# Fused attention, gated MLP and residual MLP on one core: nine of 24 head pairs transpose p on TensorE, in PSUM banks shared with the mixing MLP

## The chip, the cores and the metric

The kernel runs on one core of a Trainium2 chip. The metric is the device time of one execution in microseconds (us); the median of three runs of the kernel before is 1159.89 us (1159.18 to 1160.92). PE is TensorE, DVE is VectorE, ACT is ScalarE, POOL is GpSimd, SP is SyncE, which here issues most DMAs.

## The reference

Three stages follow each other, with B = 4 batches, S = 448 positions, H = 12 heads of D = 64, model width 768:

```python
q_n, k_n = (rmsnorm(q, g_q), rmsnorm(k, g_k))
scores = scale * np.matmul(q_n, k_n.transpose(0, 1, 3, 2))
scores = scores - np.max(scores, axis=-1, keepdims=True)
attn = np.exp(scores)
attn = attn / (np.sum(attn, axis=-1, keepdims=True) + 1e-09)
x = np.matmul(attn, v)                      # then heads side by side: [B, S, 768]

h = np.maximum(x @ w_in, 0.0)               # w_in [768, 1024]
u, v = (h[..., :d_ff // 2], h[..., d_ff // 2:])
v_n = (v - mu) / np.sqrt(var + 1e-06)
v_s = np.einsum('ts,bsd->btd', w_spatial, v_n) + b_spatial[None, :, None]
x = (u * v_s) @ w_out                       # w_out [512, 768]

xn = (x - mu) / np.sqrt(var + 1e-06) * g_ln
out = x + np.maximum(xn @ w_ch1, 0.0) @ w_ch2   # w_ch1 [768, 3072], w_ch2 [3072, 768]
```

The first stage is called attention here, the second the mixing MLP, the third the channel MLP.

## The kernel before, in words

Most products are made in f16 with each operand split into a high and a low half, so one product is three f16 products (high by high, high by low, low by high).

**Attention** goes by 24 pairs of heads, six to a batch. `att_slot` (L346) handles pair i and finishes pair i-1. `s_mm` (L231) makes the scores of a pair in four groups of two, two, two and one blocks of 128 rows (two heads of 64 rows); `softmax1` (L245) takes the row maximum on DVE (L251) and the exponential on ACT (L256), giving p in f32, unnormalised. To multiply p by v, p must be transposed. `softmax2` (L261) has two ways. For the pairs in `PE_PAIRS` (L228, pairs 0 to 5) each block of p is transposed in f32 by four PE transposes (L270) into a PSUM tile of the pool `ps_t`, and ACT copies it to SBUF (L271); `av_mm` (L284) then multiplies by v in f32 (L293). For the other pairs ACT makes the high half of p (L275), DVE the low half (L276), SP issues a DMA transpose (L278), POOL scales and splits v (L219, L221) with ACT between them (L220), and `av_mm` uses 22 f16 matmuls (L300).

`av_scale` (L304) brings 1/sum to the layout of the product: DVE multiplies the reciprocals by a 64x64 identity repeated twice (tile `dg`, L314, laid out as half, block n, row q), PE sums it over partitions (L319), ACT copies the result to `rb` (L321). `av_out` (L324) multiplies the product in PSUM by `rb` (L332); both are ordered block by block, and the result is written row by row, so both inputs are read with a step of 64 elements.

**The mixing MLP** is `moe1` (L570), one call per batch: v part (psv, L591), u part (psu, L613), spatial mixing (pss, four groups, L631 and L633), output product (pso, L650 and L660). Each group of matmuls takes one bank of the PSUM pool `ps_m`, which has two buffers; ACT or DVE empties it. Its weights are 64-bit words in DRAM that DVE decodes (L420 to L422) and splits (L397). `moe1_weights` runs beside pairs 0 to 6; `moe1` of batch b (0 to 2) beside pairs 6b+7 to 6b+12; `moe1` of batch 3 runs after attention, beside the layer norm and the first products of the channel MLP. That split is written in `merge` (L35) and the code at L1142 to L1148.

**The channel MLP** (`ffn1` L708, `ffn2` L765) follows, with its matmuls at L729 and L780 and its weight preparation at L420 to L422, L536 and L537.

**PSUM** has eight banks: `ps_x` 1, `ps_o` 1, `ps_s` 4 (two tiles of two banks), and 2 that belong to `ps_t` until pair 6's slot is over and then to `ps_m`:

```python
    c.wraw.release()
    c.ps_t.release()
    c.ps_m = ps_m = pool("ps_m", "left", 2, space=PSUM)
    c.m1 = pool("m1", "right", 1)
```

Tiles of one pool and tag take their buffers in the order in which the program names them.

**The order on each engine** is not that of the code. `issue_order` (L1056) lists all instructions, and `schedule` (L986) sorts them per engine by priorities and estimated costs. The priorities are perturbed in the steps of the table `SHAKES` (L815): seed, spread, passes. Each engine then executes its list strictly in that order.

Of the kernel before, what the change touches and what calls it, by code (L numbers as in the profile page):

```python
# [10 lines left out]
F16 = mybir.dt.float16  # L11
BF16 = mybir.dt.bfloat16
F32 = mybir.dt.float32
I32 = mybir.dt.int32
AF = mybir.ActivationFunctionType
ALU = mybir.AluOpType
AX = mybir.AxisListType
PSUM = bass.MemoryType.PSUM
DRAM = bass.MemoryType.DRAM

P = 128
B, H, S, D = 4, 12, 448, 64
NB = 7
# [131 lines left out]
def att_load(c, i):  # L155
# [9 lines left out]
    nc.sync.dma_start(out=vr[64:128, :, 0:6, :], in_=vs[:, :, 1:7, :])  # L165
    if i not in PE_PAIRS:
        nc.sync.dma_start(out=vr[64:128, :, 6, :], in_=vs[:, :, 0, :])
# [43 lines left out]
def att_v(c, i):  # L211

    nc = c.nc
    p = c.pr[i]
    if i in PE_PAIRS:
        return
# [8 lines left out]
GROUPS = ((0, 1), (2, 3), (4, 5), (6,))  # L225

CHUNKS = (0, 128, 256, S - 128)
PE_PAIRS = {0, 1, 2, 3, 4, 5}  # L228


def s_mm(c, i, g):  # L231
# [29 lines left out]
def softmax2(c, i, g):  # L261

    nc = c.nc
    p = c.pr[i]
    n = len(GROUPS[g])
    if i in PE_PAIRS:
        for j, blk in enumerate(GROUPS[g]):
            pt = c.ps_t.tile([P, 512], F32, tag="ps_t", name=f"ps_t{i}_{blk}")
            for ch, k0 in enumerate(CHUNKS):
                nc.tensor.transpose(pt[:, ch * P:(ch + 1) * P], p.pe[g][:, j, k0:k0 + P], c.ident[:])  # L270
            nc.scalar.activation(p.pT[:, blk * 512:(blk + 1) * 512], pt, AF.Copy)  # L271
        return
    x = p.pe[g][:, 0:n]
    p16 = c.att.tile([P, 2, 2, S], F16, tag="p16", name=f"p16_{i}_{g}", bufs=3)
    nc.scalar.activation(p16[:, 0:n, 0], x, AF.Copy, scale=2.0 ** 14)  # L275
    nc.vector.scalar_tensor_tensor(p16[:, 0:n, 1], x, 2.0 ** 14, p16[:, 0:n, 0], op0=ALU.mult, op1=ALU.subtract)  # L276
    b0 = GROUPS[g][0]
    nc.sync.dma_start_transpose(out=p.pT[:].bitcast(F16)[:, b0 * NB * P:(b0 + n) * NB * P].rearrange("p (c q) -> p c q", q=P),  # L278
                                in_=p16[:, 0:n].rearrange("p b t k -> p (b t k)"))


def av_mm(c, i):
# [4 lines left out]
    p.po = c.ps_o.tile([P, 512], F32, tag="ps_o", name=f"ps_o{i}")  # L287
    if i in PE_PAIRS:
        pT = p.pT.rearrange("p (b c q) -> p b c q", b=NB, c=4)
# [14 lines left out]
def av_scale(c, i):  # L304

    nc = c.nc
    p = c.pr[i]
    nc.vector.tensor_scalar(p.sm, p.sm, 1e-9, None, op0=ALU.add)
    nc.vector.reciprocal(p.sm, p.sm)
    s16 = c.small.tile([P, 2, NB], F16, tag="s16", name=f"s16_{i}", bufs=2)  # L310
    nc.vector.tensor_scalar(s16[:, 0], p.sm, 2.0 ** 15, None, op0=ALU.mult)
    nc.vector.scalar_tensor_tensor(s16[:, 1], p.sm, 2.0 ** 15, s16[:, 0], op0=ALU.mult, op1=ALU.subtract)
    dg = c.att.tile([P, 2, NB, 64], F16, tag="dg", name=f"dg{i}", bufs=1)
    nc.vector.tensor_tensor(dg.rearrange("p t n q -> p (t n) q"),  # L314
                            s16.rearrange("p t n -> p (t n)").unsqueeze(2).to_broadcast([P, 2 * NB, 64]),
                            c.eye2[:].unsqueeze(1).to_broadcast([P, 2 * NB, 64]), op=ALU.mult)
    pr = c.ps_o.tile([P, 512], F32, tag="ps_o", name=f"ps_r{i}")
    for t in range(2):
        nc.tensor.matmul(pr[:, :S], c.head, dg[:, t].rearrange("p n q -> p (n q)"), start=(t == 0), stop=(t == 1))  # L319
    p.rb = c.att.tile([P, S], F32, tag="rb", name=f"rb{i}", bufs=1)  # L320
    nc.scalar.activation(p.rb, pr[:, :S], AF.Copy, scale=2.0 ** -15 if i in PE_PAIRS else 2.0 ** -29)  # L321


def av_out(c, i):  # L324
    nc = c.nc
    p = c.pr[i]
    b, hp = i // NPAIR, i % NPAIR
    if hp == 0:
        c.xT[b] = c.xpools[b % 2].tile([P, NC6, 2, S], F16, tag="xT", name=f"xT{b}")
    xT = c.xT[b]  # L330
    x = c.att.tile([P, S], F32, tag="xo", name=f"xo{i}", bufs=1)
    nc.vector.tensor_tensor(x.rearrange("d (p n) -> d p n", n=NB), p.po[:, :S].rearrange("d (n p) -> d p n", n=NB),  # L332
                            p.rb.rearrange("d (n p) -> d p n", n=NB), op=ALU.mult)
    if i in PE_PAIRS:
        split(c, x, xT[:, hp, 0, :], xT[:, hp, 1, :], c.sv[b][:, 0:1])
    else:
        nc.scalar.activation(xT[:, hp, 0, :], x, AF.Copy)
        nc.vector.tensor_tensor(xT[:, hp, 1, :], x, xT[:, hp, 0, :], op=ALU.subtract)
    del c.pr[i]
# [6 lines left out]
def att_slot(c, i, n):  # L346
# [7 lines left out]
    if i < n:  # L354
        p = c.pr[i]
        p.ps, p.pe = {}, {}
        p.pT = c.att.tile([P, NB * 4 * P], F32, tag="pT", name=f"pT{i}", bufs=2)
        s_mm(c, i, 0)
        yield S_COST[0]
        softmax1(c, i, 0)  # L360
        s_mm(c, i, 1)
        yield S_COST[1]
        softmax1(c, i, 1)
        softmax2(c, i, 0)
    if i < n:
        s_mm(c, i, 2)
        yield S_COST[2]
        softmax1(c, i, 2)
        softmax2(c, i, 1)
    if i % 2 and i + 2 < n:  # L370
        att_front(c, i + 2, min(2, n - i - 2))
    if i > 0:
        av_scale(c, i - 1)
        av_mm(c, i - 1)
        yield AV_COST
        av_out(c, i - 1)
    if i < n:
        s_mm(c, i, 3)
        yield S_COST[3]
        softmax1(c, i, 3)  # L380
        softmax2(c, i, 2)
        softmax2(c, i, 3)
# [11 lines left out]
def split(c, raw, hi, lo, scale):  # L394

    c.nc.scalar.activation(hi, raw, AF.Copy, scale=scale)  # L396
    c.nc.vector.scalar_tensor_tensor(lo, raw, scale, hi, op0=ALU.mult, op1=ALU.subtract)  # L397
# [399 lines left out]
def weave(a, b):  # L797

    out = [iter(a), iter(b)]
    while out:  # L800
        for g in list(out):
# [10 lines left out]
WINDOW = 3413  # L812


SHAKES = ((0, 0, 2), (556, 3000, 2), (1748, 20000, 1), (1711, 1000, 3), (1453, 8000, 1), (1124, 20000, 1), (257, 300,  # L815
# [3 lines left out]


def free_size(ap):
# [225 lines left out]
def issue_order(tc):  # L1047
# [3 lines left out]
    prio = [float(o.n) for o in g.ops]  # L1051
    for seed, spread, passes in SHAKES:
        rnd = random.Random(seed)
# [13 lines left out]
def kernel(ctx: ExitStack, tc: tile.TileContext, q, k, v, g_q, g_k, w_in, w_spatial, b_spatial,  # L1067
                                   w_out, g_ln, w_ch1, w_ch2, out):
    nc = tc.nc
    c = Ctx()  # L1070
# [8 lines left out]
    def pool(name, side, bufs=1, **kw):  # L1079
        return tc.alloc_tile_pool(name=name, bufs=bufs, side=side, reuse_waits="tile", **kw)  # L1080
# [4 lines left out]
    dram = pool("dram", "left", space=DRAM)  # L1085
    c.x2d = dram.tile([B * S, DM], F32, name="x2d")
    c.ps_x = pool("ps_x", "left", 1, space=PSUM)
    c.ps_t = pool("ps_t", "left", 2, space=PSUM)
    c.ps_o = pool("ps_o", "right", 1, space=PSUM)
    c.ps_s = pool("ps_s", "right", 2, space=PSUM)  # L1090
    c.w1pool = pool("w1pool", "right")
# [9 lines left out]
    c.ones = c.const.tile([P, P], BF16, name="ones")  # L1101
    nc.vector.memset(c.ones, 1.0)

    c.ident = eye = c.wraw.tile([P, P], F32, tag="ident", name="ident", bufs=1)
    make_identity(nc, eye[:])
    c.eye2 = c.const.tile([P, 64], F16, name="eye2")
    nc.vector.tensor_tensor(c.eye2, eye[:, 0:64], eye[:, 64:P], op=ALU.add)
# [28 lines left out]
    n = B * NPAIR  # L1136
# [4 lines left out]

    merge((att(0, 7), 6 * 7000), (moe1_weights(c), 32))  # L1142
    c.wraw.release()
    c.ps_t.release()
    c.ps_m = ps_m = pool("ps_m", "left", 2, space=PSUM)
    c.m1 = pool("m1", "right", 1)
    for b in range(B - 1):
        merge((att(6 * b + 7, 6 * b + 13), 6 * 7000), (moe1(c, b), 51000))  # L1148
# [110 lines left out]
```

## Time and profile before

| | |
|---|---|
| median of three runs | 1159.89 us |
| profiled execution, own time | 1165.11 us |
| its span, first to last instruction | 1163.3 us |
| PE busy | 1051.7 us (90%) |
| DVE busy | 959.1 us (82%) |
| ACT busy | 587.3 us (50%) |
| POOL busy | 269.5 us (23%) |
| mean granted TensorE clock | 0.970 of full |

Busy time is the time in which an engine had an instruction under way. Shares over the span average over three stages that are limited by different engines, so the view by stretches has to be read beside them. The profiled execution took 5.2 us (0.45%) longer than the median of the runs.

### The profile page before, as it was taken

The page shows a single profiled execution, that of the slowest core. Times are in us where ns is not written, and L with a number is a line of the kernel's source. Part 1 is how long each engine was busy: PE and PEld are TensorE (multiplying, and loading weights), DVE is VectorE, ACT ScalarE, POOL GpSimd, SP SyncE. Part 2 cuts the span into 40 slices and gives each one's busy share as a digit, 9 for nine tenths or more (in the row PEclk, how much of TensorE's full clock was granted, in tenths as well). Part 3 has the DMA queues.
Part 4 walks back from the last instruction along what each step waited for, and adds up shares of the span by engine and source line. Part 5 has one row for each costly group of instructions (what it writes and reads, how often), then busy time and mean ns, then how long its engine had stood idle before and what let it go on. Part 6 is the DMA issues. An engine that isn't in the chain of part 4 may idle for free.

```text
span 1163.3 us, 16645 instructions
## 1 busy us (share of the span) xinstructions
PE 1051.7 (90%) x6190; PEld 543.4 (47%) x6190; DVE 959.1 (82%) x1641; ACT 587.3 (50%) x1128; POOL 269.5 (23%) x193
## 2 busy tenths in 40 slices
PE   0689579998889989897699999999999999999998
PEld 0344234444344434443355555555555555555554
DVE  7799999969997996979979788787878878787545
ACT  2899977767776884556532333142432323243110
POOL 3453653418445511222101101010110101011000
PEclk9999879999899999988899999999999999999999
DMA  7997999898999997879572222202121221110004
GB/s 240 233 234 207 189 181 190 160 233 162 205 179 212 182 166 194 183 183 250 127 195 82 82 83 58 78 28 82 34 76 66 74 78 46 65 51 32 1 28 163
DMA packets 249088, 154.46 MB, mean 133 GB/s; under 512 B 209904, under 2 KB 226224, under 8 KB 249008
## 3 DMA queue, kind: packets, MB, share of 16 engines
q1 hardware_dynamic: 244624, 142.40, 51.9%
q10 hardware_dynamic: 4384, 11.01, 3.1%
q8 instruction: 48, 0.79, 0.3%
q14 instruction: 32, 0.26, 0.1%
HBM read 86.40 MB, written 11.01 MB: 84 GB/s over the span
## 4 chain that ended last, share of the span: by engine, by line
PE 45%; DVE 8%; DMA 1%; ACT 1%; issue 1%; POOL 0%; DVEq 0%; ACTq 0%
PE ps L780 24%; PE ps1w L729 6%; PE ps1z L729 6%; PE ps1x L729 6%; PE ps1y L729 3%; DVE x L784 2%; DVE w1v L537 1%; DVE x L694 1%; DMA r_w<-in_moe_w_ch_dram 1%; DVE h L742 1%; DVE lst L681 0%; ACT r_f L525 0%; DVE r_f L422 0%; DVE r_f L421 0%; POOL rsr_x L567 0%
## 5 line engine op out<-in xcount | busy, mean ns | idle before, releaser
L780 PE MATMUL ps<-w,h 128*128 128x384 f16 x2016 | 385.9, 329 | 13.2 <-ACT w L396 5.1
L780 PEld LDWEIGHTS <-h 128*128 128x128 f16 x2016 | 197.2, 98 | 164.4 <-issue 15.1
L784 DVE SCALAR_TENSOR_TENSOR x<-ps,wio,x 128x768 f32<-128x768 f32 x168 | 169.5, 1013 | 75.2 <-PE ps L780 74.3
L729 PEld LDWEIGHTS <-w1v 128*128 128x128 f16 x1512 | 147.0, 98 | 127.4 <-issue 3.7
L240 PE MATMUL ps_s<-hT 128*64 128x448 f16 x672 | 104.4, 392 | 26.1 <-ACT pexp L256 20.3
L256 ACT ACTIVATE pexp<-ps_s,nb 128x448 f32<-128x448 f32 x168 | 106.1, 645 | 25.8 <-DVE nb L251 23.0
L528 POOL TENSOR_TENSOR sums<-r_f 128x384 f32<-128x384 f32 x12 | 12.1, 1011 | 457.7 <-ACT r_f L525 457.7
L729 PE MATMUL ps1x<-xnT,w1v 128*128 128x448 f16 x432 | 108.4, 352 | 0.2 <-DVE tc L736 0.2
L729 PE MATMUL ps1z<-xnT,w1v 128*128 128x448 f16 x432 | 106.3, 352 | 0.0
L729 PE MATMUL ps1w<-xnT,w1v 128*128 128x448 f16 x432 | 105.2, 352 | 1.0 <-DVE tu L736 0.9
L251 DVE TENSOR_REDUCE nb<-ps_s 128x2 f32<-128x896 f32 x96 | 91.8, 964 | 9.4 <-PE ps_s L240 8.9
L240 PEld LDWEIGHTS <-hT 128*64 128x64 f16 x672 | 39.6, 116 | 80.4 <-issue 53.1
L276 DVE SCALAR_TENSOR_TENSOR p<-pexp,p 128x896 f16<-128x896 f32 x72 | 72.7, 1014 | 4.6 <-ACT p L275 4.1
L185 POOL TENSOR_TENSOR rs<-ss,mhalf 128x28 f32<-128x28 f32 (+1 forms) x12 | 60.0, 4997 | 29.1 <-DVE ss L182 20.9
L203 POOL TENSOR_TENSOR qk<-raw,qk 128x896 f16<-128x896 f32 x23 | 46.1, 2005 | 78.7 <-ACT qk L202 67.5
L613 PE MATMUL psu<-xT,w_u 128*128 128x448 f16 x288 | 61.9, 357 | 2.1 <-ACT vr L595 2.0
L591 PE MATMUL psv<-w_v,xT 128*128 128x512 f16 (+1 forms) x360 | 63.5, 339 | 0.1
L275 ACT ACTIVATE p<-pexp 128x896 f16<-128x896 f32 x72 | 61.3, 857 | 2.6 <-DMA pT<-p 2.4
L741 ACT ACTIVATE h<-td 128x448 f16<-128x448 f32 x24 | 13.8, 574 | 93.1 <-DVE td L736 93.1
L650 PE MATMUL pso<-w_o,g 128*128 128x384 f16 x288 | 52.9, 327 | 1.9 <-ACT g L636 1.1
L631 PE MATMUL pss<-w_sp,vn 128*128 128x448 f16 (+1 forms) x176 | 46.7, 381 | 8.8 <-DVE u L635 7.4
L729 PE MATMUL ps1y<-xnT,w1v 128*128 128x448 f16 x216 | 53.0, 352 | 0.9 <-DMA xnT<-x 0.9
(229 smaller groups left out, 1672.3 us busy)
## 6 DMA issues: line engine op xcount, KB each, us to landing
r_w<-in_moe_w_ch_dram SPq DMA_DIRECT2D x48, 768.0 KB, 4.4
raw<-in_q_dram SPq DMA_DIRECT2D x24, 224.0 KB, 3.7
raw<-in_k_dram SPq DMA_DIRECT2D x24, 224.0 KB, 4.4
vpre<-in_v_dram SPq DMA_DIRECT2D x12, 448.0 KB, 4.8
hT<-hT SPq DMA_DIRECT2D x48, 112.0 KB, 3.1
vraw<-in_v_dram SPq DMA_DIRECT2D x24, 224.0 KB, 3.7
lv<-x2d SPq DMA_DIRECT2D x16, 336.0 KB, 4.5
x<-x2d ACTq DMA_DIRECT2D x14, 384.0 KB, 4.2
```

The costliest lines, as they stand in the source:

```text
L185: nc.gpsimd.tensor_tensor(rs, ss, c.mhalf[:, 0:14 * m], op=ALU.pow)
L240: nc.tensor.matmul(ps[hd * 64:hd * 64 + 64, :S], p.hT[:, blk, hd * 64:hd * 64 + 64], kt[:, :, hd * 64:hd * 64 + 64], start=(t == 0), stop= ...
L251: nc.vector.tensor_reduce(nb[:, 0:n], ps[:, 0:n, :S], axis=AX.X, op=ALU.max, negate=True)
L256: nc.scalar.activation(pe[:, j, :], ps[:, j, :S], AF.Exp, bias=nb[:, j:j + 1], scale=1.0, accum_out=p.sm[:, blk:blk + 1])
L275: nc.scalar.activation(p16[:, 0:n, 0], x, AF.Copy, scale=2.0 ** 14)
L276: nc.vector.scalar_tensor_tensor(p16[:, 0:n, 1], x, 2.0 ** 14, p16[:, 0:n, 0], op0=ALU.mult, op1=ALU.subtract)
L591: nc.tensor.matmul(ps[m * h:m * h + m, 0:hn], xT[:, k, x, t * P:t * P + m], wv[:, w, k, h * hn:(h + 1) * hn], start=(n == 0), stop=(n == l ...
L613: nc.tensor.matmul(ps[:, :S], wu[:, w, k, f * P:(f + 1) * P], xT[:, k, x, :], start=(n == 0), stop=(n == len(mms) - 1))
L650: nc.tensor.matmul(ps[:, 0:384], g16[:, f, g, s0:s0 + m], wo[:, w, f, e * 384:(e + 1) * 384], start=(n == 0), stop=(n == len(mms) - 1))
L729: nc.tensor.matmul(ps, w[:, a, x, d], xnT[:, :, 21 * y + 3 * b + d], start=first and n == 0, stop=n == 8, skip_group_check=True)
L780: nc.tensor.matmul(ps[:, e, 0:QK], h16[:, f, x, t * P:(t + 1) * P], w2[:, y, f, e * QK:(e + 1) * QK], start=n == 0, stop=n == 5)
L784: nc.vector.scalar_tensor_tensor(x2, ps[:, :, 0:QK], io[:, 0:1], x2, op0=ALU.mult, op1=ALU.add)
```

## The change

`PE_PAIRS` gains pairs 6, 12 and 18, the first pairs of batches 1, 2 and 3 in the order of the work. Their transposes would need `ps_t` while `moe1` needs `ps_m`; so `ps_t` goes, `ps_m` is allocated from the start, and the transposes and `moe1` take turns in its two buffers, in the order of the program. The f32 identity moves from the weight pool to `const`, as it is now needed for longer. `dg` is laid out as half, row q, block n; the multiplication that makes it reads the 14 reciprocals with step one and the identity as the repeated element. `rb` then comes out in the row order in which L332 writes, so L332 reads it with step one and only the PSUM operand with a step of 64. `SHAKES` is another table, of 15 steps instead of 23, so the order on every engine is another. Line numbers after the change are lower by one from L314 on, by two or more from L1088 on.

```diff
-PE_PAIRS = {0, 1, 2, 3, 4, 5}
+PE_PAIRS = {0, 1, 2, 3, 4, 5, 6, 12, 18}
...
-            pt = c.ps_t.tile([P, 512], F32, tag="ps_t", name=f"ps_t{i}_{blk}")
+            pt = c.ps_m.tile([P, 512], F32, tag="ps_m", name=f"ps_t{i}_{blk}")
...
-    dg = c.att.tile([P, 2, NB, 64], F16, tag="dg", name=f"dg{i}", bufs=1)
-    nc.vector.tensor_tensor(dg.rearrange("p t n q -> p (t n) q"),
-                            s16.rearrange("p t n -> p (t n)").unsqueeze(2).to_broadcast([P, 2 * NB, 64]),
-                            c.eye2[:].unsqueeze(1).to_broadcast([P, 2 * NB, 64]), op=ALU.mult)
+    dg = c.att.tile([P, 2, 64, NB], F16, tag="dg", name=f"dg{i}", bufs=1)
+    nc.vector.tensor_tensor(dg, s16[:].unsqueeze(2).to_broadcast([P, 2, 64, NB]),
+                            c.eye2[:].unsqueeze(1).unsqueeze(3).to_broadcast([P, 2, 64, NB]), op=ALU.mult)
...
-        nc.tensor.matmul(pr[:, :S], c.head, dg[:, t].rearrange("p n q -> p (n q)"), start=(t == 0), stop=(t == 1))
+        nc.tensor.matmul(pr[:, :S], c.head, dg[:, t].rearrange("p q n -> p (q n)"), start=(t == 0), stop=(t == 1))
...
-                            p.rb.rearrange("d (n p) -> d p n", n=NB), op=ALU.mult)
+                            p.rb.rearrange("d (p n) -> d p n", n=NB), op=ALU.mult)
...
-SHAKES = ((0, 0, 2), (556, 3000, 2), (1748, 20000, 1), (1711, 1000, 3), (1453, 8000, 1), (1124, 20000, 1), (257, 300,
+SHAKES = ((0, 0, 6), (1368, 300, 1), (577, 8000, 1), (1518, 3000, 1), (439, 1000, 1), (1820, 40000, 3), (267, 8000,
...
-    c.ps_t = pool("ps_t", "left", 2, space=PSUM)
+    c.ps_m = ps_m = pool("ps_m", "left", 2, space=PSUM)
...
-    c.ident = eye = c.wraw.tile([P, P], F32, tag="ident", name="ident", bufs=1)
+    c.ident = eye = c.const.tile([P, P], F32, name="ident")
...
-    c.ps_t.release()
-    c.ps_m = ps_m = pool("ps_m", "left", 2, space=PSUM)
```

Two places of the new order matter for the prediction. In these rows hT16 is the transposed q and k of pair 16, ps_s16_3 the last group of its scores, ps_t18_3 the transposed fourth block of pair 18, and pss1_2 the third of four spatial mixing groups of batch 1.

PE before, at the end of that mixing group of batch 1:

```order
L631 LDWEIGHTS vn16_1_2756
L631 MATMUL pss1_2_3794<-w_sp_1094,vn16_1_2756 128x448
L633 LDWEIGHTS ones_96
L633 MATMUL pss1_2_3794<-bias3_1349,ones_96 128x448
L240 LDWEIGHTS hT16_3145
L240 MATMUL ps_s16_3_3456<-hT16_3145 64x448
```

PE with the change, at the start of the same group:

```order
L240 LDWEIGHTS hT18_3497
L240 MATMUL ps_s18_3_3832<-hT18_3497 64x448
L270 MATMUL ps_t18_3_3771<-ident_98,pexp18_1_3736 128x128 x2
L630 LDWEIGHTS vn16_1_2780
L630 MATMUL pss1_2_3815<-w_sp_1093,vn16_1_2780 128x448
```

The group stood ahead of the last scores of pair 16; now it stands behind the last scores of pair 18 and the transposes of that pair's first four blocks, two pairs further on in attention.

DVE at the start of the program, one piece of the difference (v0_w0 is the first 64-bit weight block, gk the gain of k, which comes by DMA):

```order
+L419 TENSOR_SCALAR v0_f_257<-v0_w0_258 128x512
+L420 SCALAR_TENSOR_TENSOR v0_f_257<-v0_w0_258,v0_f_257 128x512
 L114 TENSOR_TENSOR gg_118<-gg_118,gk_117 128x64
-L1128 TENSOR_TENSOR gm0_222<-gln_219 128x6
-L471 TENSOR_TENSOR bq_1334<-bp_1332 64x7
+L1126 TENSOR_TENSOR gm0_222<-gln_219 128x6
+L421 SCALAR_TENSOR_TENSOR v0_f_257<-v0_w0_258,v0_f_257 128x512
 L116 TENSOR_REDUCE gam_122<-gg_118 128x1
```

The first two operations of the weight decode now stand ahead of the product of the gains; the weight's DMA is SP's first issue.

## Rows read from the trace of the kernel before

**Rows 1.** Busy time by stretches: length, then busy us of each engine, clock, DMA.
```profile
58.00:116.00 58.00, 52.12 (x297) 24.02 (x293) 55.73 (x93) 53.60 (x122) 25.20 (x13) 0.94 0.88 221
116.00:160.00 44.00, 25.14 (x149) 12.01 (x148) 42.58 (x79) 38.35 (x76) 21.94 (x15) 0.73 0.94 190
160.00:247.00 87.00, 86.02 (x535) 38.07 (x535) 78.09 (x132) 63.85 (x134) 37.88 (x25) 1.00 0.94 181
247.00:261.00 14.00, 14.00 (x87) 5.50 (x82) 8.21 (x12) 10.44 (x21) 2.26 (x3) 1.00 1.15 252
261.00:350.00 89.00, 78.41 (x516) 35.90 (x514) 85.00 (x134) 66.99 (x138) 51.64 (x31) 0.94 0.94 181
350.00:380.00 30.00, 28.39 (x191) 13.76 (x189) 22.59 (x33) 20.04 (x41) 17.83 (x10) 1.00 1.03 207
380.00:440.00 60.00, 54.41 (x359) 23.78 (x356) 59.13 (x103) 48.05 (x104) 17.93 (x13) 1.00 0.96 177
440.00:470.00 30.00, 29.06 (x197) 15.10 (x196) 19.41 (x45) 13.89 (x22) 5.08 (x6) 1.00 0.76 203
470.00:516.00 46.00, 40.17 (x205) 18.29 (x204) 42.99 (x89) 27.93 (x42) 11.79 (x10) 0.89 0.74 162
516.00:590.00 74.00, 56.57 (x291) 28.85 (x290) 68.01 (x136) 38.40 (x52) 11.27 (x12) 0.88 0.79 186
590.00:1163.00 573.00, 567.32 (x3272) 318.02 (x3270) 433.47 (x684) 174.55 (x322) 43.79 (x40) 1.00 0.21 70
```

**Rows 2.** Costliest groups by form: splitting and transposing p, DVE, ACT and PE.
```profile
L276 DVE SCALAR_TENSOR_TENSOR p<-pexp,p 128x896 f16<-128x896 f32 x54 | 60.2, 1119 | 2.4 <-ACT p L275 2.0
L276 DVE SCALAR_TENSOR_TENSOR p<-pexp,p 128x448 f16<-128x448 f32 x18 | 12.5, 697 | 2.2 <-ACT p L275 2.2
L271 ACT ACTIVATE pT<-ps_t 128x512 f32<-128x512 f32 x42 | 26.9, 664 | 0.7 <-PE ps_t L270 0.7
L270 PE MATMUL ps_t<-ident,pexp 128*128 128x128 f32 x168 | 30.9, 310 | 5.4 <-ACT pT L271 3.9 <-ACT pexp L256 1.4
L270 PEld LDWEIGHTS ps_t<-ident,pexp 128*128 128x128 f32 x168 | 20.1, 153 | 22.1 <-ACT pT L271 11.3 <-issue 8.0 <-ACT pexp L256 1.5
L293 PE MATMUL ps_o<-pT,vraw 128*64 128x448 f32 (+1 forms) x96 | 24.7, 552 | 0.3 <-ACT pT L271 0.3
L300 PE MATMUL ps_o<-pT,v 128*64 128x448 f16 x396 | 50.7, 368 | 0.6 <-ACT rb L321 0.6
```

**Rows 3.** The same view: scaling the output on DVE, and an operation of the channel MLP.
```profile
L332 DVE TENSOR_TENSOR xo<-ps_o,rb 128x448 f32<-128x448 f32 x24 | 22.2, 926 | 10.1 <-PE ps_o L300 9.9
L736 DVE SCALAR_TENSOR_TENSOR tq<-ps1y,tp 128x448 f32<-128x448 f32 x24 | 14.9, 622 | 16.3 <-ACT tp L749 11.4 <-PE ps1y L729 4.8
```

**Rows 4.** One line's instructions, L314: duration ns min, median, max.
```profile
L314 DVE TENSOR_TENSOR dg<-s,eye x24: 1069/1082/2771, 51.9 to 437.9; 128x896 f16<-128x896 f16 x24
```

**Rows 5.** Instructions in order of time on DVE, start of the program: start, us.
```profile
6.62 0.22 DVE L114 TENSOR_TENSOR gg<-gg,gk 128x64 f32<-128x64 f32 x1 [4.93 <-DMA gk<-in_g_k_dram]
...
8.77 0.42 DVE L420 TENSOR_SCALAR v_f<-v_w 128x512 int32<-128x512 int32 x1
9.22 0.69 DVE L421 SCALAR_TENSOR_TENSOR v_f<-v_w,v_f 128x512 int32<-128x512 int32 x1
```

**Rows 6.** The same view on PE: last scores of pairs 16 and 18, start of batch 2's psv.
```profile
319.29 0.57 PE L240 MATMUL ps_s<-hT 128*64 128x448 f16 x4
...
347.48 1.14 PE L240 MATMUL ps_s<-hT 128*64 128x448 f16 x10
...
354.18 2.11 PE L591 MATMUL psv<-w_v,xT 128*128 128x512 f16 x9
```

**Rows 7.** Costliest groups: spatial mixing and output product of the mixing MLP on PE.
```profile
L631 PE MATMUL pss<-w_sp,vn 128*128 128x448 f16 (+1 forms) x176 | 46.7, 381 | 8.8 <-DVE u L635 7.4 <-ACT u L616 0.7 <-DVE vn L605 0.7
L650 PE MATMUL pso<-w_o,g 128*128 128x384 f16 x288 | 52.9, 327 | 1.9 <-ACT g L636 1.1 <-ACT x2o L653 0.5 <-DVE u L635 0.2
L660 PE MATMUL pso<-w_o,g 128*64 128x384 f16 x96 | 11.5, 332 | 1.3 <-DVE g L637 1.3
```

More of the change, by code (lines that the diff above doesn't have):

```diff
@@ L812 @@
 WINDOW = 3413
-SHAKES = ((0, 0, 2), (556, 3000, 2), (1748, 20000, 1), (1711, 1000, 3), (1453, 8000, 1), (1124, 20000, 1), (257, 300,
[3 rows of a table removed]
+SHAKES = ((0, 0, 6), (1368, 300, 1), (577, 8000, 1), (1518, 3000, 1), (439, 1000, 1), (1820, 40000, 3), (267, 8000,
+          1), (505, 300, 3), (827, 8000, 1), (1565, 8000, 3), (426, 20000, 2), (1065, 20000, 1), (1830, 1000, 3),
+          (631, 1000, 1), (625, 40000, 2))
 def free_size(ap):
```

3 rows, old and new, of the table SHAKES are left out of this document.

## The prediction

> **What bounds the kernel now.** I read the busy time by stretches first [rows 1], since one share for the whole span mixes three stages. Compare PE and DVE with each stretch's length. From 58 to 160 us, attention beside the weights, DVE is busy for 55.7 of 58 and 42.6 of 44 us; PE has slack, 18.9 of the 44 in the second stretch. From 160 to 261, PE is busy for 100.0 of 101 us and DVE for 86.3: PE sets the pace. From 261 to 350 it is DVE again (85.0 of 89, PE 78.4); from 350 to 380 PE (28.4 of 30, DVE 22.6); from 380 to 440 DVE (59.1 of 60). From 470 to 590 DVE leads (111.0 of 120, PE 96.7) with decoding and splitting the channel MLP's weights, which starts when attention has given up its memory. From 590 on PE is busy for 567.3 of 573 us: rigid, and touched by the change only through its order. So the change matters by how much sooner 590 comes. DVE is nearly full wherever PE is not, but each has stretches in which it waits for the other. DMA is busy at 0.74 to 1.15 up to 590, yet what ACT and DVE wait for in the rows of the p path is mostly each other [rows 2].
>
> **The change, part by part.** Times are us, against the profiled execution's own 1165.1.
>
> *The split of p on DVE goes, for three pairs.* Per pair, three operations of 1.119 and one of 0.697 [rows 2]: 4.05, three times. What it is worth depends on the stretch. Pair 6 runs in 116 to 160, where DVE is full: -4.05. Pair 12 falls in 160 to 261, where DVE has 14.7 idle: 0. Pair 18 falls, in the new order, in the DVE-bound 261 to 350 instead of at its end (below): -4.05.
>
> *PE gets more.* Per pair, transposes 30.9/6 = 5.15 and f32 products 24.7/6 = 4.12, less f16 products 50.7/18 = 2.82 [rows 2]: +6.45. Pair 6's lies in the 18.9 that PE idles in 116 to 160, where the granted clock averages 0.73, between its levels of 1.2 and 2.4 GHz, behind waits of PE: 0. Pair 12's lies in the full stretch: +6.45. Pair 18's is hidden by the 10.6 idle of 261 to 350; without that cover it would cost 6.45 too. PE also waits for ACT's copies between transposes: from 5.4/6 = 0.9 a pair by the matmuls' row to 11.3/6 = 1.9 by the weight loads' [rows 2]. For two pairs I take the low end, as the matmuls are what others wait for: +1.8.
>
> *ACT, POOL, SP, memory: nothing.* ACT's seven copies of 0.664 a pair [rows 2] are 4.65, against two passes that go; it idles 22.0 of the 89 in 261 to 350 [rows 1]. POOL loses its scaling and its subtraction; four DMA transposes and one small load leave SP's queue per pair, with nothing late because of them. The identity's new place moves no instruction of weight.
>
> *dg, laid out anew.* Now 1.08 for 896 elements [rows 4], one element a step. No row shows the new pattern. Half of that would be the lower end; for the upper, L332 pays (0.926 - 0.622)/448 = 0.68 ns an element for its steps [rows 3], which on 896 would be +0.61. I take no change, as one operand still repeats its elements and both keep their size. For 24 pairs the ends are -13.0 and +14.6.
>
> *L332 with one strided operand instead of two.* It takes 0.926; an operation of the same size, PSUM and SBUF both read in order, takes 0.622 [rows 3]. So a pair gains between 0 and 0.30. Whether PSUM or SBUF costs it, no row tells; I take half, 0.15, for the 18 of 24 pairs outside the PE-bound stretches: -2.75. The Trainium skill (Vector Engine (DVE) Microarchitecture Reference, Measured stream behaviour on trn2) speaks against this: a stream that hops at every element costs 1.73 ns a column with one source hopping, 1.76 with both. By it the 24 pairs would gain 0.03 x 448 x 24 ns = 0.3 in all, an estimate. No run here shows either.
>
> *The start.* DVE idles 4.93 until the gains arrive [rows 5]. Two weight operations (0.42 and 0.69) now stand ahead of that: -1.1. That weight's DMA goes ahead of pair 0's loads, but as many bytes lie before them as did.
>
> *The order in the middle.* Sharing banks ties attention to `moe1`: the third mixing group of batch 1 must follow the first four transposed blocks of pair 18. In the trace of before, pair 16's last scores, which followed that group, begin at 319.3; pair 18's end at 348.6 [rows 6]. So attention has to run some 29 earlier against the mixing MLP, or the mixing MLP waits. The former fills DVE where it idles now: 5.8 in 247 to 261, 7.4 in 350 to 380 [rows 1]. I take half, -6.6, between 0 and all 23.8 with the 10.6 of 440 to 470. What `moe1` lags behind by then, PE can make up: it idles 8.1 between 350 and 470 and 23.3 between 470 and 590, where an earlier end of attention lets the weights come sooner.
>
> The sum: -4.05 - 4.05 + 6.45 + 1.8 - 2.75 - 1.1 - 6.6 = -10.3, so 1154.8 for an execution like the profiled one. That one stands 5.2 above the median: **1149.6, say 1150**.
>
> **The rivals.**
>
> *DVE sets everything up to 590.* Then all it loses counts: 12.15 + 7.3 (24 x 0.30) + 1.1 = 20.6, which gives 1139. For it: the five DVE-bound stretches. Against: PE's 100.0 of 101 in 160 to 261. Chance 0.18.
>
> *The order gives nothing and L332 keeps its price.* -10.3 + 6.6 + 2.75 = -0.95: 1159, no change. This is a change that does less than it says: the pairs' splits go, and nothing overlaps better. Chance 0.15. L332 keeping its price, with the rest as forecast, is a rival too: 1152, at one half within each other case, as 0.926 fits either reading; it is what the skill's rule on hopping streams would do here.
>
> *The shared banks hold the mixing MLP back.* If attention doesn't come forward, batch 1's third group waits until pair 18's last scores, at 348.6 less some 7 won until there (1.1, 4.05 and 12 x 0.15). Behind it PE has two mixing groups (46.7/8 = 5.8), the output product ((52.9 + 11.5)/4 = 16.1) [rows 7] and three of pair 18's seven blocks (2.2), so batch 2's psv begins at 365.7 instead of 354.2 [rows 6]: +11.5, 1171. It decides once pair 18's last scores end after 354.2 - 24.1 = 330. For it: batch 1's group stands two pairs further on, and DVE has only 4 idle in 261 to 350 to bring attention forward. Against: the slack from 350 to 590 named above. A dearer dg would end on the same side. Chance 0.27.
>
> **How the numbers follow.** The forecast has 0.40, around 1150 from 1143 to 1157 (its waits, the half for L332 and the order's own ends). A measurement of this kernel can tell about 0.2%, 2.3 us. Faster is the forecast with the first rival, 0.58; same 0.15; slower 0.27. The range goes from 1138, just below the DVE-bound case, to 1168, which leaves out about half of the last rival and little at the low end.
>
> **What would show it.** Right: the low-half operation 60 times instead of 72 and 252 transposes instead of 168; the start of PE's full stretch some 5 us before 160; psv of batch 2 no later than 354; PE full from some 580 on, not 590. L332 near 0.77 would fit my half, 0.92 no gain, 0.63 a penalty on SBUF alone. dg at 1.08. Wrong: new idle time of PE ahead of the mixing groups or the transposes of pairs 12 and 18, released by ACT's exponentials or copies; batch 2's psv after 360 with the stretch from 470 to 590 no shorter; dg well above 1.1. If the time is lower but the point at which PE fills has not moved, the reason lies in the channel MLP's order, which I cost at nothing.

## The result, and the profile after

The change takes a median of **1146.99 us** (1145.16 to 1147.93, four runs) against 1160.41 us for the kernel before on the same chip: ratio 0.9877, 95% interval 0.9849 to 0.9904. The profiled execution took 1147.5 us with a span of 1145.7; the mean granted clock rose from 0.970 to 0.987. Below, differences between kernels are worked out from such ratios, times 1160 us; two ratios with intervals of this width tell about 4 us apart.

The view by stretches of the kernel after (length, then busy us of PE, PEld, DVE, ACT, POOL; clock, DMA share, GB/s) stands against [rows 1]:

```profile
58.00:116.00 58.00, 52.63 (x317) 25.43 (x315) 54.95 (x100) 57.42 (x132) 27.12 (x14) 0.97 0.89 223
116.00:160.00 44.00, 39.00 (x221) 16.47 (x221) 42.69 (x85) 44.00 (x96) 27.93 (x15) 0.96 0.85 188
160.00:247.00 87.00, 81.46 (x525) 38.68 (x524) 72.12 (x125) 64.40 (x133) 39.63 (x23) 0.98 0.91 186
247.00:261.00 14.00, 14.00 (x88) 6.19 (x87) 12.11 (x16) 11.24 (x23) 8.58 (x7) 1.00 0.83 185
261.00:350.00 89.00, 86.39 (x574) 40.99 (x573) 80.89 (x137) 70.25 (x146) 47.79 (x26) 1.00 0.95 182
350.00:380.00 30.00, 30.00 (x202) 14.74 (x201) 22.53 (x36) 21.36 (x45) 12.90 (x12) 1.00 0.89 179
380.00:440.00 60.00, 58.89 (x377) 27.54 (x376) 48.80 (x96) 39.57 (x82) 8.25 (x8) 1.00 0.81 173
440.00:470.00 30.00, 29.65 (x171) 14.76 (x170) 28.64 (x63) 18.18 (x25) 6.28 (x8) 1.00 0.78 185
470.00:516.00 46.00, 38.01 (x204) 18.18 (x205) 37.04 (x76) 24.62 (x40) 8.53 (x8) 0.96 0.80 170
516.00:590.00 74.00, 61.74 (x308) 31.79 (x308) 67.33 (x132) 34.14 (x50) 12.28 (x10) 0.88 0.83 201
590.00:1145.00 555.00, 550.44 (x3182) 309.55 (x3179) 416.95 (x661) 169.92 (x314) 44.31 (x40) 1.00 0.19 63
```

Length less PE's busy time is what PE idles. It fell from 18.9 to 5.0 in 116 to 160, from 10.6 to 2.6 in 261 to 350, from 8.1 to 1.5 in 350 to 470 and from 23.3 to 20.3 in 470 to 590; it rose from 1.0 to 5.5 in 160 to 261. From 58 to 590 that makes 27.5 less. PE's busy time rose by 9.2 (1051.7 to 1060.9), so the span fell by 17.6 (the rest lies outside these stretches). The channel MLP's first product began at 497.7 instead of 515.6 and its second at 519.3 instead of 537.0, 17.7 earlier; the way from the second product's 300th matmul to the end of the span is 517.2 long, against 517.1: all of the gain is made before the channel MLP. Up to the second product's first matmul PE idles 70.3 us instead of 95.2. DVE idles 70.1 instead of 62.3, but it is busy for 449.2 instead of 474.7.

The groups of the parts that changed, from the view of the costliest groups by form (count, busy us, mean ns, then the idle time before them and what ended it), answer to [rows 2 to 4]:

```profile
L276 DVE SCALAR_TENSOR_TENSOR p<-pexp,p 128x896 f16<-128x896 f32 x45 | 52.4, 1165 | 1.1 <-ACT p L275 0.8
L276 DVE SCALAR_TENSOR_TENSOR p<-pexp,p 128x448 f16<-128x448 f32 x15 | 11.9, 790 | 0.3 <-ACT p L275 0.2
L270 PE MATMUL ps_t<-ident,pexp 128*128 128x128 f32 x252 | 44.5, 298 | 5.5 <-ACT pT L271 2.8 <-ACT pexp L256 2.2
L300 PE MATMUL ps_o<-pT,v 128*64 128x448 f16 x330 | 42.3, 359 | 0.2 <-ACT rb L320 0.2
L331 DVE TENSOR_TENSOR xo<-ps_o,rb 128x448 f32<-128x448 f32 x24 | 14.8, 615 | 3.1 <-PE ps_o L293 2.7 <-PE ps_o L300 0.3
L314 DVE TENSOR_TENSOR dg<-s,eye 128x896 f16<-128x896 f16 x24 | 27.7, 1156 | 0.1
```

The low half runs 60 times, the transposes 252 times. The operation that was L332 is L331 now: 615 ns instead of 926 [rows 3]. dg's median has not moved (1082 both times). PE in order of time, at the two places that the prediction spoke of:

```profile
321.49 0.57 PE L240 MATMUL ps_s<-hT 128*64 128x448 f16 x3
321.99 0.44 PE L270 MATMUL ps_t<-ident,pexp 128*128 128x128 f32 x2
322.26 0.92 PE L630 MATMUL pss<-w_sp,vn 128*128 128x448 f16 x4
...
355.30 0.60 PE L590 MATMUL psv<-w_v,xT 128*128 128x512 f16 x2
```

Pair 18's last scores end at 322.1, 26.5 before [rows 6], and the mixing group behind them starts at 322.3 without a hole; batch 2's psv is at 355.3, where it was at 354.2. In the rows of DVE in order of time, the first group of pair 18's row maxima moved from 344.0 to 315.1. So attention came forward by 27 to 29 us there, while the mixing MLP went back a little: that third group of batch 1 ends 5.7 us later (325.0 instead of 319.4), batch 2's psv begins 1.1 later. Last, PE's waits from 116 to 440 (us in total, times, longest); before:

```profile
PE ps_s L240 <- ACT pexp L256: 19.7, 16, 3.8
```

and after:

```profile
PE ps_s L240 <- ACT pexp L256: 5.7, 6, 2.7
```

Scores wait for a free PSUM tile, which ACT's exponential releases after DVE's row maxima. This wait, 14 us of it, is the largest single one that went.

### The profile page after: what moved, and what is told of

Read it like the earlier page. It is cut to its first block, busy times and chain, and to the rows that moved or that the text cites. A ratio compares the mean times of both kernels' runs of the same rounds, so it can differ in the third digit from the quotient of the medians.

```text
span 1145.7 us, 16730 instructions
## 1 busy us (share of the span) xinstructions
PE 1060.9 (93%) x6256; PEld 553.8 (48%) x6256; DVE 930.2 (81%) x1629; ACT 585.3 (51%) x1134; POOL 267.0 (23%) x187
## 4 chain that ended last, share of the span: by engine, by line
PE 50%; DVE 4%; POOL 0%; issue 0%; ACT 0%; DVEq 0%
PE ps L779 27%; PE ps1x L728 6%; PE ps1z L728 6%; PE ps1w L728 6%; PE ps1y L728 3%; DVE x L783 1%; DVE x L693 1%; DVE w1v L536 0%; POOL rsr_x L566 0%; DVE lst L680 0%; DVE r_f L420 0%; ACT x L695 0%; DVE h L741 0%; DVE lv L704 0%; DVE lv L703 0%
## 5 line engine op out<-in xcount | busy, mean ns | idle before, releaser
L256 ACT ACTIVATE pexp<-ps_s,nb 128x448 f32<-128x448 f32 x168 | 108.4, 666 | 29.3 <-DVE nb L251 26.6
L527 POOL TENSOR_TENSOR sums<-r_f 128x384 f32<-128x384 f32 x12 | 14.4, 1199 | 427.7 <-ACT r_f L524 340.5
L276 DVE SCALAR_TENSOR_TENSOR p<-pexp,p 128x896 f16<-128x896 f32 (+1 forms) x60 | 64.2, 1071 | 1.4 <-ACT p L275 1.0
L185 POOL TENSOR_TENSOR rs<-ss,mhalf 128x28 f32<-128x28 f32 (+1 forms) x12 | 57.7, 4810 | 15.0 <-DVE ss L182 7.1
L275 ACT ACTIVATE p<-pexp 128x896 f16<-128x896 f32 (+1 forms) x60 | 51.5, 873 | 1.0 <-DMA pT<-p 0.8
L748 ACT ACTIVATE tp<-ps1x 128x448 f32<-128x448 f32 x24 | 12.9, 538 | 76.0 <-PE ps1x L728 76.0
```

Of the source, the lines that this page charges most:

```text
L185: nc.gpsimd.tensor_tensor(rs, ss, c.mhalf[:, 0:14 * m], op=ALU.pow)
L256: nc.scalar.activation(pe[:, j, :], ps[:, j, :S], AF.Exp, bias=nb[:, j:j + 1], scale=1.0, accum_out=p.sm[:, blk:blk + 1])
```

## Experiments

Those whose label begins with x keep the changed kernel's order: each engine's list is written out, and what an edit adds is put in where its inputs are due in that order; nothing else trades places, but for some twenty instructions in the run with the whole preparation of p. The others are sorted by the table named; with the layout alone edited, the sort gives the same lists.

**The layout undone in the change.** dg and the scaling as before, all else as after.

```diff
-    dg = c.att.tile([P, 2, 64, NB], F16, tag="dg", name=f"dg{i}", bufs=1)
+    dg = c.att.tile([P, 2, NB, 64], F16, tag="dg", name=f"dg{i}", bufs=1)
...
-                            p.rb.rearrange("d (p n) -> d p n", n=NB), op=ALU.mult)
+                            p.rb.rearrange("d (n p) -> d p n", n=NB), op=ALU.mult)
```

> The changed kernel with dg, rb and L331 as before; the order on every engine is that of the changed kernel, row by row. Theory (the strided read of rb cost 0.31 us a pair on an engine that is nearly full): L331 back at 0.92 from 0.615, 7.4 us of DVE for 24 pairs, of which those of 18 pairs count: 1147 + 5.5 = 1152 to 1153. Rival 1 (these 7.4 us lie beside PE work): 1147 to 1149. Rival 2 (delays add up behind an order fixed for shorter ones): 1157 or more, all of the gain of the change.

Measured: 1151.36 us, ratio 0.9930 (0.9907 to 0.9952), 6 us slower than the change. The groups by line:

```profile
L314 DVE TENSOR_TENSOR dg<-s,eye 128x896 f16<-128x896 f16 x24 | 28.5, 1186 | 0.1
L331 DVE TENSOR_TENSOR xo<-ps_o,rb 128x448 f32<-128x448 f32 x24 | 22.3, 928 | 3.1 <-PE ps_o L293 2.7 <-PE ps_o L300 0.3
```

24 x (928 - 615) ns are 7.5 us of DVE, and by the ratios most of that is on the path (6 us, give or take 4).

**The layout alone, in the kernel before.** The same edit the other way round.

> The kernel before with the new layout of dg alone; the order on every engine is that of before, row by row. Theory: L332 falls to 0.615, 5 to 6 us of the 7.4 reach the end: 1154 to 1155. Rival 1 (hidden): 1159 to 1160. Rival 2 (the layout is the whole change): 1148 or less.

Measured: 1158.32 us, ratio 0.9988 (0.9973 to 1.0004), between what the theory and the first rival asked for. The operation takes the same as in the change:

```profile
L332 DVE TENSOR_TENSOR xo<-ps_o,rb 128x448 f32<-128x448 f32 x24 | 14.7, 613 | 9.9 <-PE ps_o L300 9.9
```

So the same 7.5 us are worth 1.4 in the old order and 6 in the new. The intervals of the two values overlap a little. The idle time before the operation may be why: DVE waits 9.9 us for PE's product there, 3.1 with the change, so time that it saves is partly waited away.

**Six pairs, sorted by the new table.**

```diff
-PE_PAIRS = {0, 1, 2, 3, 4, 5, 6, 12, 18}
+PE_PAIRS = {0, 1, 2, 3, 4, 5}
```

> The changed kernel with pairs 6, 12 and 18 back on the DMA way; shared banks, dg and the table of 15 steps stay, the order is sorted anew from that table. Theory (pairs 6 and 18 save 4 us of DVE each where DVE is full): slower than the change by 5 to 9 us, 1152 to 1156, with psv of batch 0 starting later by 4 us or more. Rival (the pairs trade DVE for PE and give nothing; table and layout are the change): 1145 to 1149.

Measured: 1188.06 us, ratio 1.0249 (1.0222 to 1.0275), above both ranges. A table steers a random search, so another program gets another order from it, here a bad one. This run says nothing of the pairs, and is the reason why the later ones keep the order.

**Nine pairs, sorted by the old table.**

```diff
-SHAKES = ((0, 0, 6), (1368, 300, 1), (577, 8000, 1), (1518, 3000, 1), (439, 1000, 1), (1820, 40000, 3), (267, 8000,
+SHAKES = ((0, 0, 2), (556, 3000, 2), (1748, 20000, 1), (1711, 1000, 3), (1453, 8000, 1), (1124, 20000, 1), (257, 300,
...
```

> The changed kernel with the old table of 23 steps; nine pairs, shared banks and dg stay, the order is sorted anew. Theory (the new table brings some 3 of the 13 us): 1149 to 1153. Rival 1 (any order does, pairs and layout are the change): 1146 to 1148. Rival 2 (the table carries the change): 1156 to 1162.

Measured: 1161.92 us, ratio 1.0021 (1.0001 to 1.0041), 17 us slower than the change. Three more pairs and the new layout give nothing without an order that fits them. The other way round is open: no run searched for a better order of the six pairs, so how much of the gain such a search alone would bring is not shown.

**One pair, or all three, taken back, order kept.** The edits, one for each kernel:

```diff
-PE_PAIRS = {0, 1, 2, 3, 4, 5, 6, 12, 18}
+PE_PAIRS = {0, 1, 2, 3, 4, 5, 12, 18}
+PE_PAIRS = {0, 1, 2, 3, 4, 5, 6, 18}
+PE_PAIRS = {0, 1, 2, 3, 4, 5, 6, 12}
+PE_PAIRS = {0, 1, 2, 3, 4, 5}
```

Without pair 6: 

> The changed kernel with pair 6 alone back on the DMA way. The order of the changed kernel is kept for every instruction that both programs have; the 40 new ones stand where their inputs are due by that order. Theory (DVE is full there, PE is not): slower than the change by 3 to 5 us, 1150 to 1152. Rival 1 (hidden): within 1.5 us of 1147. Rival 2 (what counts is the length of pair 6's chain, since psv of batch 0 waits behind it): slower by 8 us or more.

Without pair 12: 

> The same with pair 12 alone back on the DMA way. Theory of the prediction (pair 12 costs 6.45 us of PE in a stretch where PE is full, and saves DVE nothing): faster than the change by up to 6 us, 1141 to 1146. Rival 1 (no effect): 1146 to 1148.5. Rival 2 (its DVE relief counts): 1150 or more.

Without pair 18: 

> The same with pair 18 alone back on the DMA way. Theory of the prediction (DVE-bound stretch, the relief of 4 us counts): 1150 to 1152. Rival (the trace of after has PE busy for 130 of 133 us from 247 to 380, so PE is the bound there now and gets 6 us back): 1141 to 1146.

Without all three: 

> The same with all three pairs back on the DMA way: six pairs in the order of the changed kernel, banks and layout as changed. Theory of the prediction (-4.05 for each of pairs 6 and 18, +6.45 + 1.8 for pair 12): slower by 0 to 4 us, 1147 to 1151. Rival 1 (order, banks and layout are all of it): 1145 to 1149 with each single pair within 1.5 us too. Rival 2 (the pairs make the new alignment possible at all): 1155 or more.

Measured: 1161.38 without pair 6 (ratio 0.9990, 0.9976 to 1.0005), 1152.29 without pair 12 (0.9912, 0.9888 to 0.9937), 1160.93 without pair 18 (1.0007, 0.9988 to 1.0027), 1181.81 without all three (1.0166, 1.0143 to 1.0189). In the new order the pairs are worth 13, 4 and 15 us, and 33.5 together: they add up. Each value is above the prediction's. Pair 12's 4 us are at the edge of what two ratios tell apart; in the profile of the run without it the first row maxima are some 6 us late from pair 14 on. In any case the gain of up to 6 us that was expected from taking it back did not come. These are prices in this order and with these places for the instructions put in; the run without all three is slower than the kernel before.

Without pair 6 neither engine is full in its stretch, and the clock has fallen; the second block is of the waits there:

```profile
116.00:160.00 44.00, 30.07 (x155) 12.08 (x154) 36.67 (x75) 33.96 (x70) 23.31 (x12) 0.77 0.82 168
```

```profile
PE ps_r L318 <- DVE xo L331: 6.7, 2, 4.1
ACT v L220 <- POOL vraw L219: 6.5, 1, 6.5
PE ps_o L300 <- ACT rb L320: 6.0, 1, 6.0
```

ACT stands at the high half of v (L220) until POOL has scaled it; the copy to `rb` is behind that in ACT's list, and PE's next product behind the copy. Without pair 12, PE stands once at that pair's product, 4.7 us, for v: the load lands at 232.4, POOL's scaling and ACT's high half follow, and PE starts at 234.4:

```profile
PE ps_o L300 <- DMA vraw<-in_v_dram: 4.7, 1, 4.7
```

And without pair 18 the wait for exponentials in 116 to 440 is back at nearly what it was before:

```profile
PE ps_s L240 <- ACT pexp L256: 17.2, 11, 5.7
```

More than half of it lies between 314 and 336. There ACT stands at the high half of p for a buffer that a DMA transpose still reads, and exponentials stand behind that in its list; the change has no such wait there:

```profile
ACT p L275 <- DMA pT<-p: 8.5, 3, 3.8
```

These are three different places of one chain, the old way's preparation of p and v.

**DVE's share of it, and a control.** All nine pairs stay on PE; pairs 6, 12 and 18 also get the four DVE operations each of the old way, into a tile that nothing reads. The control has the same twelve instructions in the same places, with 8 columns of each block.

```diff
             nc.scalar.activation(p.pT[:, blk * 512:(blk + 1) * 512], pt, AF.Copy)
+        if i in EXTRA:
+            x = p.pe[g][:, 0:n]
+            e16 = c.att.tile([P, 2, 2, S], F16, tag="p16", name=f"e16_{i}_{g}", bufs=3)
+            nc.vector.scalar_tensor_tensor(e16[:, 0:n, 1], x, 2.0 ** 14, x, op0=ALU.mult, op1=ALU.subtract)
         return
```

> The changed kernel in its own order, pairs 6, 12 and 18 on the matrix engine as there, and on top of it the twelve VectorE operations of the old way (one for each group of query blocks, low half of p, about 1.0 us each, 12 us in all) writing a tile that nothing reads. Theory A (VectorE's load is what the pairs paid for, the prediction's account): pairs 6 and 18 lose their 4 us each again or more, 1155 to 1165. Theory B (SP's in-order queue and the latency of the chain are the price, not the load): VectorE has the room, 1147 to 1151.

The control: 

> The control of the run with twelve VectorE operations on top: the same twelve instructions in the same places of every queue, with the same waits and the same buffers, but on 8 columns of each block instead of 448 (some 0.1 to 0.2 us each instead of about 1.2). If VectorE's time is what cost 16 us there: 1145 to 1150, that is 13 us or more below it. If the place in the order, the waits or the p buffers taken were the cost: 1157 to 1165, as there.

Measured: 1163.15 us (ratio 1.0025, 1.0003 to 1.0046) and for the control 1152.06 (0.9919, 0.9889 to 0.9949). The added operations in the first, by form:

```profile
L276 DVE SCALAR_TENSOR_TENSOR e<-pexp 128x896 f16<-128x896 f32 x9 | 11.5, 1273 | 4.6 <-DMA pT<-p 3.9 <-ACT pexp L257 0.7
L276 DVE SCALAR_TENSOR_TENSOR e<-pexp 128x448 f16<-128x448 f32 x3 | 3.5, 1153 | 0.0
```

and in the control:

```profile
L276 DVE SCALAR_TENSOR_TENSOR e<-pexp 128x8 f16<-128x8 f32 x3 | 1.7, 568 | 0.0
L276 DVE SCALAR_TENSOR_TENSOR e<-pexp 128x16 f16<-128x16 f32 x9 | 1.6, 173 | 6.1 <-DMA pT<-p 5.0 <-ACT pexp L257 1.2
```

Between the two lie 11.7 us of DVE time (15.0 less 3.3), and by the ratios 12.3 us of the kernel's, give or take 4: **in this order DVE's time counts in full**, as far as these ratios tell. By the first row maxima of a pair, beyond the 1.3 us that the two profiled executions differ by at pair 0, 6.7 us of it are lost by pair 8, 9.8 by pair 12 and 11.8 by pair 18: more than half at pair 6. The control itself is 5 us slower than the change, between its two ranges. Its row maxima are 0.1 behind the change's at pair 18 and 5.3 at pair 19; in between DVE waits for a p buffer that a DMA still holds (4.0 of the 5.0 us in its row), the wait that ACT has without pair 18: an operation that takes almost no time has a price by its waits alone. By this, about a third of the 33.5 us is DVE's time; what remains is the rest of the chain, as the waits above suggest, but no run shows it by itself. The next one was meant to.

**The whole old preparation of p on top, unread.** As above, with ACT's high half and SP's four transposes a pair, into buffers shared with squares of q and k.

```diff
+            nc.scalar.activation(e16[:, 0:n, 0], x, AF.Copy, scale=2.0 ** 14)
+            nc.vector.scalar_tensor_tensor(e16[:, 0:n, 1], x, 2.0 ** 14, e16[:, 0:n, 0], op0=ALU.mult, op1=ALU.subtract)
+            eT = c.att.tile([P, 14, D], F32, tag="sq", name=f"eT{i}_{g}", bufs=2)
+            nc.sync.dma_start_transpose(out=eT[:].bitcast(F16).rearrange("p a d -> p (a d)")[:, 0:n * NB * P].rearrange("p (c q) -> p c q", q=P),
```

> As before, but with the whole preparation of p of the old way for pairs 6, 12 and 18: ScalarE's high half, VectorE's low half and the four DMA transposes a pair on SP's queue, into a tile that nothing reads; TensorE waits for none of it. Theory A (VectorE's load): the same as with the VectorE operations alone, within 2 us. Theory B (SP's in-order queue stands behind the transposes, and the next pairs' loads behind it): 1156 to 1170, with the row maxima of pair 8 at 146 or later instead of 140.4. Theory C (the price is TensorE's own wait at the end of the chain, on p and v): under 1152 for both kernels, though the three pairs together were worth 35 us.

Measured: 1194.73 us, ratio 1.0300 (1.0272 to 1.0329), slower than with none of the three pairs on PE, and above every range. The buffers spoil it. `v_scale` loads v into the same two; one of its loads, issued at 104.65 with the change, now stands with two more behind the transposes on SP:

```profile
131.19 3.90 SPq L279 DMA_TRANSPOSE eT<-e  x2
135.74 4.92 SPq L141 DMA_DIRECT2D vpre<-in_v_dram  x3
```

ACT waits 9.9 us for that load, and the copies of pT behind it keep PE's banks. The run shows once more that a late instruction on an in-order queue is dear, but it lies above theory B's range and doesn't price the transposes: inconclusive. (The expectation's mark was misread: 140.4 is the row maximum of pair 7's last block; pair 8's first come at 147.5 with the change and at 173.7 here.)

**A tenth pair.** Pair 7 as well, order kept.

```diff
-PE_PAIRS = {0, 1, 2, 3, 4, 5, 6, 12, 18}
+PE_PAIRS = {0, 1, 2, 3, 4, 5, 6, 7, 12, 18}
```

> A tenth pair, 7, in the same stretch as pair 6, on the matrix engine; all else in the changed kernel's order. Theory (between 116 and 160 TensorE was busy 39 of 44 us, VectorE 42.7): TensorE takes 6.5 us more and fills its 5 us of holes, later pairs come 3 to 10 us earlier: 1143 to 1148. Rival (TensorE is the bound with 93% busy and each further pair costs its 6.5 us, as pair 12 was forecast to): 1151 to 1155.

Measured: 1163.41 us, ratio 1.0026 (1.0006 to 1.0046), 17 us slower than the change and worse than the rival. Its first stretch, then the waits from 116 to 195:

```profile
116.00:160.00 44.00, 38.76 (x228) 16.95 (x225) 37.09 (x74) 38.09 (x83) 23.32 (x12) 1.00 0.57 130
```

```profile
PEld ps_t L270 <- ACT pT L271: 9.7, 13, 1.1
DVE nb L251 <- PE ps_s L240: 9.4, 3, 4.3
```

With the change the first of these is 4.6 us. Now DVE idles 6.9 of 44 us and waits for scores, 4.3 us of it at 144.4: these stand in PE's list behind three blocks' transposes, each of which waits 0.69 us for ACT to empty one of the two shared banks. So the shared banks can hold something back, though here it is attention and not the mixing MLP of the third rival. Most of the loss comes later: the first row maxima are 3.2 us behind the change's at pair 8 and 15.1 at pair 9, and no run shows which wait carries that. None of these kernels beats the change.

## Why the prediction was right, and where its terms were not

The time lies in the forecast's own range (1143 to 1157), with its sign and a gain of 13.4 us by the medians against 10.3. The sum is nearer than its terms, and that is in part luck: errors of both signs cancelled.

- **PE's extra work was right.** Transposes +13.6 us (44.5 - 30.9), the f32 products +14.2 (38.9 - 24.7), the f16 products -8.4: +19.4 against 3 x 6.45 = 19.35. All of PE's busy time rose by 9.2 only; other groups took a little less, and matmuls of groups that alternate overlap.
- **The split's 12.15 of DVE came out as 8.4** (72.7 to 64.3), since the operations that are left take longer, 1165 instead of 1119 ns and 790 instead of 697. Against that, 7.1 us that stand in no term went from L200, which the change doesn't touch: 24 operations with medians of 1080 and 1085 ns, of which the longest took 4.39 us before and 1.82 after.
- **The order in the middle moved attention as the step said, but what it filled was PE.** Attention's last scores of pair 18 came forward by 26.5 us, where 29 were asked for, and the mixing MLP went back by 1 to 6. DVE's idle time was filled in 247 to 261 (5.8 to 1.9) and in 440 to 470 (10.6 to 1.4), not in 350 to 380, and it grew in 160 to 247 (8.9 to 14.9) and in 380 to 440 (0.9 to 11.2). Up to the second product PE's idle time fell by 24.9 and DVE's rose by 7.8. The third rival's point (last scores after 330) was not reached, by 8 us.
- **"Pair 12 falls in 160 to 261, where DVE has 14.7 idle: 0", and PE +6.45, is not what the runs show.** Taking it back gains nothing; it costs 4 us, at the edge of what two ratios tell apart. Idle time summed over a stretch doesn't show the one place where PE stands 4.7 us for v.
- **Pairs 6 and 18 at 4.05 were too low by a factor of three or more**, 13 and 15 us in the order kept. The first rival priced the splits of all three pairs at 12.15, every microsecond of DVE counted; runs show 12.3, give or take 4, for 11.7.
- **"ACT, POOL, SP, memory: nothing" failed.** I compared busy times. What the pairs also lose is a chain of five engines and queues whose late links stop in-order queues, as ACT behind POOL in the run without pair 6.
- **The order as a term of its own, -6.6, is the step that let errors cancel.** New order with six pairs: 1181.8. Old order by its table with nine: 1161.9. Both together: 1147.0. Pairs and order can't be priced apart; the low terms for the pairs and the absent price for an order that doesn't fit them hid each other.
- **L332's half was too careful.** 615 ns: with the step left on the PSUM operand alone all of the penalty is gone, 0.31 an operation and not 0.15. By the ratios it is worth 6 us in the new order, where I took 2.75, and 1.4 in the old. In the Trainium skill (Vector Engine (DVE) Microarchitecture Reference, Measured stream behaviour on trn2) one source that hops at every element costs 1.73 ns a column, both 1.76 and none 1.054. Those rows stand under the access granule of SBUF, and I applied them to an operand in PSUM: with only that one hopping the operation takes what L736 takes with none (622) [rows 3]. The step on the SBUF operand, 0.69 ns a column here, is near the 0.68 that one source costs by that section (1.73 less 1.054, an estimate).
- **dg at no change was right** (median 1082 both times). The start gave 0.4 (first row maxima at 38.36 instead of 38.79), not 1.1. PE's waits for ACT's copies fell by the matmuls' row (3.9 to 2.8 of ACT pT) and grew by 4.1 by the weight loads' (11.3 to 15.4), for 1.8 taken.
- **Two marks were set too narrowly.** Batch 0's psv begins 22 us earlier (159.8 to 137.9), not 5; batch 2's is 1.3 past the 354 that I named, with a faster kernel. PE is full from some 560 on (19.6 of 20 us to 580, 11.2 before), sooner than the 580 named.

## What to carry to other kernels

Where several engines are each nearly full and execute fixed lists, price a removed chain by the waits that it ends as well as by the busy time that it frees: one in-order queue that stops passes its delay to all. A change of work and the order made for it are one term; test the parts with the order held, and put a control with empty operations beside an added load. Before charging strided access to an operation, ask for each operand which memory it lies in.

## What was not expected of the hardware

On DVE, a step of 64 f32 elements on a PSUM operand alone shows no price (613 to 615 ns for 448 columns, against 622 for L736, which has none); with the step on the SBUF operand too the operation takes 0.31 us more (926 to 928). No run has the step on the SBUF operand alone. And in the run with added DVE operations one of them took 2.78 us instead of 1.08, here in order of time on DVE,

```profile
123.64 2.78 DVE L276 SCALAR_TENSOR_TENSOR e<-pexp 128x896 f16<-128x896 f32 x1
```

and on POOL:

```profile
122.85 2.61 POOL L203 TENSOR_TENSOR qk<-raw,qk 128x896 f16<-128x896 f32 x1
```

It ends at 126.42, 0.96 after POOL's operation. The Trainium skill (SBUF — State Buffer, SBUF: two separate sides) says that VectorE with two SBUF inputs and GpSimd exclude each other for a whole instruction; this trace agrees. A DVE operation moved beside one of POOL's can thus cost 1.7 us more than its median says. L200's longest before the change, 4.39 us from 289.99 on, is of this kind: two of POOL's operations follow each other beside it, and it ends 0.95 after the second.
